# A planned order of work laid down with other lengths, and P V sets that may run in two halves

## The chip, the cores and the metric

The kernel runs on one core of a Trainium2 chip. The core has five engines with queues of their own: TensorE (PE in the profile, with PEld for its weight loads) for matmuls, ScalarE (ACT) for exponentials, VectorE (DVE) and GpSimd (POOL) for elementwise work, and SyncE (SP), which issues most DMAs. Matmuls write to PSUM, eight banks of 512 fp32 columns. The metric is the device time of one execution in microseconds. A difference of under about 0.2% can't be told from no change.

## The reference

Two attention blocks over the same input x (2048 tokens, 512 wide, 32 heads of 16) are mixed by a gate:

```python
x = A_x
g = _sigmoid((x * gate_w).sum(-1, keepdims=True))
# A: softmax attention
q, k, v = split((x @ A_wqkv))                       # 32 heads of 16
p = _softmax(einsum("bhqd,bhkd->bhqk", q, k) * 16 ** -0.5)
a = einsum("bhqk,bhkd->bhqd", p, v) @ A_wo
# B: linear attention
phi = lambda t: where(t > 0, t + 1, exp(t)) + 1e-6
num, den = phi(q) @ (phi(k)^T v), phi(q) . sum(phi(k))
b = (num / (den + 1e-6)) @ B_wo
return g * a + (1 - g) * b
```

Nearly all of the work is A's: 32 heads of 2048 x 2048 scores, each put through an exponential, and the product of the exponentials with V (called P V here).

## The kernel before, in words

**Units, groups and rounds.** The scores of a head are computed transposed: keys on the partitions, 512 queries along the columns. One unit is 128 keys by 512 queries of one head and fills one PSUM bank. A round is four heads by 512 queries, 64 units; there are 32 rounds, so 2048 units. Four 32-row strips of the array hold one head each, so one pass of PE (tiles `Qpad`, `KT`, line 685, where every matmul is issued) gives the scores of two to four units at once. ACT takes two banks at a time in one call (1024 columns, line 2063), and sometimes three (1536) or one (512). There are two slots of three banks each (`SLOTS`), used in turn: while ACT reads one, PE fills the other. The stretch of PE's work between two passes is called a gap here.

**Claims.** The third unit of a pass mostly isn't ACT's. It is claimed (`claim`): VectorE turns the scores into an integer whose bits are an approximate exponential (line 1565), and two more copies with an added step come from GpSimd (line 1609) or VectorE (line 1606). Three products with weighted V stand for the one exponential, so a claimed unit costs PE three products instead of one and ACT nothing. `MIN_LEFT`, `CLAIM_LOAD`, `RING_LOAD`, `STARVE` and `LATE` say when a claim may be made and when another step goes first.

**P V.** The products run in sets of four (`pv_cols`): four matmuls of 32 columns of weights, one for each head of the round, side by side in the array, 512 queries each, all into one accumulator bank. After the 64 units' worth of a round (`acc_n` reaches 64) the bank is copied out (`oraw`, line 1306), normalised, and another bank takes the next round. The last round runs in another form, full array and 52 columns, for a short end.

**Steps.** Everything else of PE (projections of Q, K and V, all of block B, the output products) is cut into steps and pieces that are put into gaps by `misc_step`, when their target group is due. Their results are evicted by VectorE, those with an exponential by ACT too (`epool`, line 970). The projection of Q, the normalisation, the transposes of B's output and the outputs issue DMAs on SP's queue.

**The order is written by a planner.** The program is straight-line code for each engine, in an order that the Python code plans as it records. It keeps a clock for each engine (`PE.t`, `AC.t`, `DV.t`, `PO.t`) from assumed lengths: `SET_T` of a set, `MM512` of a 512-wide matmul, `QK_T` of a pass, `SWITCH_T` where PE changes the way in which the array is divided, and so on. Nothing of these lengths is in the program: on the chip each engine runs its order as fast as its semaphores allow. A length that is off only puts work where it doesn't fit. After each pass the loop at lines 2092 to 2106 fills the gap:

```python
t_late = max(t_lim, AC.t - (QK_T + SWITCH_T + ROWS_SEEN + LAT + MARGIN))
...
room = min(MOST, int((t_late - PE.t - enter) / SET_T + ROOM))
if behind and room > 0 and pv_step(PE.t, most=room, least=3):
    continue
```

`t_late` is the latest time at which the next pass should come so that ACT doesn't run dry; `t_lim` is when its banks come free. `room` is the number of sets that fit, where a set may reach over the end by up to `ROOM` of its length. `least` is how many of the four columns of a set must be filled. `behind` is whether many exponentials wait for their product. Then steps have their turn, then sets again. If PE has nothing to do before `t_lim`, and too little was multiplied lately, `fill` puts in a matmul with zeros (`warm`), which keeps the clock of the array up.

Of the kernel before, what the change touches and what calls it, by code (L numbers as in the profile page):

```python
# [17 lines left out]
STATS = {}  # L18
# [167 lines left out]
LAT = 0.11  # L186
SET_T = 0.218
MM512 = 0.216
QK_T = 0.324
# [4 lines left out]
PV_MAC = 0.087  # L194
SWITCH_T = 0.095
SELF_T = 0.08
# [16 lines left out]
def bass_gated_mix__mha_block__linear_attn_block__prompt_kernel(  # L213
# [30 lines left out]
    PRE_GAP = 6  # L244
    OUT_GAP = 6

    with ExitStack() as es:
# [194 lines left out]
        ADD_W = 0.4  # L442
        YIELD = 1.2
        YIELD_SOON = 0.5
        POOL_TT = 1.3
# [892 lines left out]

        def pv_cols(now, r, force, want, most, least):

# [16 lines left out]
            sets = []  # L1357
            while len(sets) < most:
                s = [q[0] for q in by_j if q]
                full = sum(1 for j in range(4) if by_j[j] or left_j[j] == 0)  # L1360
                if not s or (full < least and not (force and any(e in first for e in s))):
                    break
                for q in by_j:
                    if q:
                        q.popleft()
                sets.append(s)
# [3 lines left out]
            t8 = rounds[r][0]  # L1370
            fns, rds = [], []
            for s in sets:
                STATS["sets"] = STATS.get("sets", 0) + 1
                STATS["in_sets"] = STATS.get("in_sets", 0) + len(s)
                for e in s:
# [10 lines left out]
                    for res in (e[3], vr):  # L1386
                        if res not in rds:
                            rds.append(res)
                    acc_n[0] += e[4]
                    done_j[(r, j)] = done_j.get((r, j), 0) + e[4]  # L1390
                    pv_pending.remove(e)
            pe_macro(fns, reads=rds, writes=[r_acc], dur=SET_T * len(sets), mac=0.2 * len(sets), mode="cols")
            fresh[0] = False
            if acc_n[0] == NU:
# [30 lines left out]

        def pv_step(now, force=False, want=None, most=3, least=4):

# [16 lines left out]
            if r < NR - 1 or part[0] == 0:  # L1444
                return pv_cols(now, r, force, want, most, least)
            if add_part(False):
                return True
            most = PV_UNITS * most
            sel = []
# [67 lines left out]

        MIN_LEFT = 14
        MIN_LEFT_LAST = 20
# [99 lines left out]
        GPR = 14.8  # L1619
        B0 = 0.4  # L1620
        B1 = 21
# [208 lines left out]
        FORCE_N = 1  # L1830
        MOST = 4
        OVER = 0.15
        FIRST_T = 0.43
        ROOM = 0.6
        CLAIM_LOAD = 3.2
        LATE_CLAIM = 4
        STARVE = 5
        MAC_LOW = 0.45
# [3 lines left out]
        END_FROM = 44  # L1842
        RING_LOAD = 4
        RING_LATE = 4
        BEHIND = 30
        LEND = 140
        RES_FROM = 60
        MARGIN = 0.19
        PV_LAG = 14
        LATE = 12  # L1850
        LAG_END = 12
# [128 lines left out]
        while True:  # L1980
# [112 lines left out]
            while PE.t < t_lim - 0.05:  # L2093
                pump(PE.t)
                behind = sum(1 for e in pv_pending if e[3] in r_PT) > (PV_LAG if act_round[0] < NR - 1 else LAG_END)
                enter = SWITCH_T if pe_mode[0] == "full" else 0.0
                room = min(MOST, int((t_late - PE.t - enter) / SET_T + ROOM))
                if behind and room > 0 and pv_step(PE.t, most=room, least=3):
                    continue
                if g > last_stage and misc_step(PE.t, t_late):  # L2100
                    continue
                if not behind and room > 0 and pv_step(PE.t, most=room):
                    continue
                if PE.t + FILL_T < t_lim and mac_until(max(t_lim, PE.t + FILL_AHEAD)) < (MAC_END if acc_n[0] >= END_FROM else MAC_LOW) and fill(PE.t):
                    continue
                PE.t += 0.05
# [248 lines left out]
```

## Time and profile before

| What | us |
|---|---|
| Time of the runs: median (lowest to highest) | 675.98 (675.3 to 675.98) |
| The profiled execution's own time | 675.2 |
| Its span, first to last instruction | 673.4 |
| ACT busy | 660.0 |
| PE busy | 655.0 |
| DVE busy | 576.0 |
| POOL busy | 550.8 |

The span is 1.8 us shorter than the execution's own time, which includes what lies around it. Busy time counts a moment once in which two calls of one engine overlap. So a busy engine may still be late: ACT's calls are longer in the records than the time from one to the next. For PE the ends of matmuls are modelled; starts are recorded. In the rows of groups and of the timeline, what stands in square brackets or behind the bar is the idle time just before, with what ended it.

### The profile page before, as it was taken

To read this page: it belongs to the slowest core of one execution; us is meant where nothing else is said; L and a number is where in the kernel's file an instruction comes from. 1 tells how busy PE (TensorE), PEld (TensorE's weight loads), DVE (VectorE), ACT (ScalarE), POOL (GpSimd) and SP (SyncE) were. 2 spreads that over 40 slices of the span, in tenths; PEclk is the share of its full clock that TensorE was granted. 3 is DMA by queue.
4 is the path that set the end of the run, shared out by engine and by line. 5 is a ranking of instruction groups with operands and counts; after the bars stand their busy time and mean duration, and the time that the engine had idled before them with its cause. 6 is when DMAs were issued, how large, how long until landed. Compare 5 with 4: busy or idle time off the path is not lost.

```text
span 673.4 us, 19207 instructions
## 1 busy us (share of the span) xinstructions
PE 655.0 (97%) x8078; PEld 200.1 (30%) x8080; DVE 576.0 (86%) x968; ACT 660.0 (98%) x715; POOL 550.8 (82%) x311
## 2 busy tenths in 40 slices
PE   8999999999999999999999999999999999999997
PEld 4322223333223232333222323323322222222223
DVE  4589889889887886888988998999889998989894
ACT  6999999999999999999999999999999999999995
POOL 5098889887889997788986999778788888898883
PEclk9999999999999999999999999999999999999999
DMA  9900101001010021101001010010211401010011
GB/s 221 252 3 12 24 2 31 6 11 27 1 35 2 18 50 35 32 2 29 7 10 35 10 41 11 16 29 13 46 26 24 52 25 42 10 44 24 20 41 44
DMA packets 44816, 22.96 MB, mean 34 GB/s; under 512 B 33976, under 2 KB 40568, under 8 KB 44728
## 3 DMA queue, kind: packets, MB, share of 16 engines
q1 hardware_dynamic: 42712, 20.12, 13.5%
q10 hardware_dynamic: 2016, 1.57, 0.9%
q8 instruction: 66, 1.08, 0.7%
q14 instruction: 22, 0.18, 0.1%
HBM read 8.00 MB, written 2.10 MB: 15 GB/s over the span
## 4 chain that ended last, share of the span: by engine, by line
ACT 95%; PE 4%; DMA 1%; DVE 1%; issue 0%; ACTq 0%
ACT PT L2063 92%; PE ps L685 3%; ACT epool L970 2%; DMA PT<-in_A_x_dram 1%; DVE DP L2165 0%; DVE xT L1909 0%; PE ps L692 0%; DVE KT L859 0%; DVE DP L2170 0%; DVE flag L2175 0%; ACT eg L954 0%; ACTq L2278 0%
## 5 line engine op out<-in xcount | busy, mean ns | idle before, releaser
L2063 ACT ACTIVATE PT<-ps 128x1024 bf16<-128x1024 f32 (+1 forms) x675 | 648.1, 1155 | 0.7 <-PE ps L685 0.5
L1609 POOL TENSOR_TENSOR DP<-DP,step 128x1024 int32<-128x1024 int32 x278 | 527.0, 1925 | 99.1 <-DVE DP L1565 27.6
L1565 DVE TENSOR_SCALAR DP<-ps 128x512 int16<-128x512 f32 x654 | 433.0, 685 | 69.1 <-PE ps L685 62.9
L685 PE MATMUL ps<-Qpad,KT 32*128 32x512 bf16 x2048 | 264.6, 384 | 10.0 <-ACT PT L2063 4.7
L685 PE MATMUL ps<-DP,Vaug 128*32 128x512 f16 x1949 | 206.8, 384 | 1.6 <-DVE oraw L1306 0.7
L685 PE MATMUL ps<-PT,Vaug 128*32 128x512 bf16 x1384 | 174.3, 384 | 0.6 <-DVE Vaug L914 0.5
L685 PEld LDWEIGHTS ps<-Qpad,KT 32*128 32x128 bf16 x2048 | 66.6, 91 | 269.9 <-ACT PT L2063 242.9
L685 PEld LDWEIGHTS ps<-DP,Vaug 128*32 128x32 bf16 x1949 | 49.7, 94 | 66.2 <-issue 41.1
L685 PEld LDWEIGHTS ps<-PT,Vaug 128*32 128x32 bf16 x1384 | 42.1, 95 | 46.7 <-issue 36.7
L685 PE MATMUL ps<-warm 128*32 128x512 bf16 (+1 forms) x272 | 46.7, 387 | 1.1 <-POOL step L735 1.1
L1606 DVE TENSOR_SCALAR DP<-DP 128x2048 int16<-128x2048 int16 (+1 forms) x50 | 33.4, 696 | 0.0
L685 PE MATMUL ps<-xT,wA 128*32 128x512 bf16 x432 | 32.6, 384 | 0.0
L1294 POOL TENSOR_TENSOR OT<-oraw,rbc 128x512 bf16<-128x512 f32 x12 | 15.6, 1302 | 11.3 <-DVE DP L1606 5.4
L970 ACT ACTIVATE epool<-ps 128x512 bf16<-128x512 f32 x32 | 23.4, 731 | 0.0
L1306 DVE COPY oraw<-ps 128x512 f32<-128x512 f32 x31 | 21.2, 682 | 0.7 <-PE ps L685 0.6
L685 PE MATMUL ps<-xT,wB 128*32 128x512 bf16 x256 | 19.7, 384 | 0.0
L685 PE MATMUL ps<-wB,xT 128*32 128x512 bf16 x256 | 19.3, 384 | 0.0
L685 PE MATMUL ps<-woA,OT 128*32 128x512 bf16 (+1 forms) x226 | 19.1, 384 | 0.0
L975 DVE SCALAR_TENSOR_TENSOR phi<-ps,epool 128x512 bf16<-128x512 f32 x24 | 16.3, 681 | 0.0
L685 PEld LDWEIGHTS ps<-warm 128*32 128x32 bf16 (+1 forms) x272 | 11.6, 98 | 13.8 <-issue 12.1
L859 DVE CAST KT<-ps 128x512 bf16<-128x512 f32 (+1 forms) x16 | 10.7, 667 | 5.2 <-PE ps L685 5.2
L685 PE MATMUL ps<-wA,xT 128*128 128x128 bf16 x192 | 14.9, 220 | 0.0
(106 smaller groups left out, 244.4 us busy)
## 6 DMA issues: line engine op xcount, KB each, us to landing
rbc<-oraw SPq DMA_DIRECT2D x16, 256.0 KB
OT<-in_A_x_dram SPq DMA_DIRECT2D x4, 512.0 KB, 7.1
Qpad<-Qs SPq DMA_DIRECT2D x124, 16.0 KB, 1.8
oraw<-oraw SPq DMA_DIRECT2D x60, 32.0 KB, 1.9
wA<-in_A_wqkv_dram SPq DMA_DIRECT2D x1, 1536.0 KB, 7.7
wB<-in_B_wqkv_dram SPq DMA_DIRECT2D x1, 1536.0 KB, 8.6
out_dram<-outt SPq DMA_DIRECT2D x12, 128.0 KB, 1.7
phi<-in_A_x_dram ACTq DMA_DIRECT2D x3, 256.0 KB, 6.1
```

What stands on the lines that cost most here:

```text
L685: return lambda: nc.tensor.matmul(o, lhsT=l, rhs=r, start=start, stop=stop, skip_group_check=sg)
L859: push(1, [(lambda: nc.vector.tensor_copy(KT[:, par, c0:c1], src), [r_bank[b]], [r_KT[par][t]], d_psum(n), None)])
L970: op(AC, lambda: nc.scalar.activation(epool[:, s, :], bank_ap(b), ACT.Exp), reads=[r_bank[b]], writes=[r_e[s]], dur=0.6, issue=0.48)
L975: (lambda: nc.vector.scalar_tensor_tensor(out=dst, in0=bank_ap(b), scalar=0.0, in1=epool[:, s, :], op0=ALU.max, op1=ALU.add), [r_bank[b], ...
L1294: push(1, [(lambda: (nc.gpsimd if on_pool else nc.vector).tensor_tensor(OT[:, t8, 512 * qc:512 * (qc + 1)], oraw[:, 0, :], rbc[:], ALU.mul ...
L1306: push(0, [(lambda: nc.vector.tensor_copy(oraw[:, half, :], acc), [r_acc], [r_oraw[half]], d_psum(512), evicted)])
L1565: push(0 if in_group else 1, [(lambda: nc.vector.tensor_scalar(DP[:, i, 512 * k:512 * (k + 1)].bitcast(I16), bank_ap(b), FRAC - Y_BIAS4, Y ...
L1606: ops = (lambda z=z, i2=i2, y=y, n=n: nc.vector.tensor_single_scalar(DP[:, i2, 0:n].bitcast(I16), y, STEPS[z], ALU.add), mine_, out_, d_sb ...
L1609: ops = (ops[0], mine_ + [r_step], out_, ops[3], None, POOL_ADD, lambda z=z, i2=i2, y=DP[:, i, 0:n].bitcast(I32), n=n: nc.gpsimd.tensor_te ...
L2063: op(AC, lambda p0=p0, b0=b0, n=n: nc.scalar.activation(PT[:, 512 * p0:512 * p0 + n], ps[:, 512 * b0:512 * b0 + n], ACT.Exp, scale=LN2 / F ...
```

## The change

The assumed lengths of a set, of a 512-wide matmul and of a switch are set to other values, and with them some twenty thresholds of the planner, so the whole order comes out anew. A set of P V may be run as two halves of 256 columns: where no whole set fits (`room` is 0) but 0.12 us less 40% do, `pv_cols` issues the first half and keeps the second in `split`, which runs when P V has its next turn. Only when the second half is issued are the products counted. The second call of `pv_step` in the loop no longer needs `behind` to be false, and takes sets with three filled columns where a whole set fits. `count` and `ended` hold what stood at the end of `pv_cols` before.

In numbers of the order that is laid down: 676 passes in place of 675, ACT calls of three, two and one banks 48, 628 and 0 in place of 45, 629 and 1, claims 648 in place of 654, P V sets 890 in place of 869, of which 103 run as halves, and filler groups 71 in place of 116.

```diff
--- before.py
+++ after.py
@@ -184,15 +184,15 @@
 
 
 LAT = 0.11
-SET_T = 0.218
-MM512 = 0.216
+SET_T = 0.223
+MM512 = 0.222
 QK_T = 0.324
 
 PVW = 26
 WIDE_MAC = 0.4
 PV_T = 0.1012
 PV_MAC = 0.087
-SWITCH_T = 0.095
+SWITCH_T = 0.104
 SELF_T = 0.08
 ROWS_SEEN = 0.0
 ACT_END = 0.25
@@ -242,7 +242,7 @@
     KV0, KV1 = 1.0, 1.2
     PRE_T = 5
     PRE_GAP = 6
-    OUT_GAP = 6
+    OUT_GAP = 4
 
     with ExitStack() as es:
         _cnt = [0]
@@ -440,8 +440,8 @@
         port_ev = [None]
         boost = [None]
         ADD_W = 0.4
-        YIELD = 1.2
-        YIELD_SOON = 0.5
+        YIELD = 1.8
+        YIELD_SOON = 0.3
         POOL_TT = 1.3
         POOL_V = 0.9
         POOL_ADD = 1.97
@@ -1336,7 +1336,19 @@
         done_j = {}
         PV_UNITS = 2
 
-        def pv_cols(now, r, force, want, most, least):
+        split = []
+        HALF_T = 0.12
+        ROOM_H = 0.4
+
+        def pv_cols(now, r, force, want, most, least, half=False):
+
+            if split:
+                s, fns, rds = split.pop()
+                pe_macro(fns, reads=rds, writes=[r_bank[acc_bank[0]]], dur=HALF_T, mac=0.1, mode="cols")
+                count(r, s)
+                return ended(r)
+            if half and most == 0 and len(started) < 4:
+                return False
 
             urgent = sum(1 for e in pv_pending if e[3] in r_PT) > PT_URGENT
             mine = [e for e in pv_pending if e[0] == r]
@@ -1355,7 +1367,7 @@
                 by_j[e[1] % 4].append(e)
             left_j = [16 - done_j.get((r, j), 0) - sum(e[4] for e in by_j[j]) for j in range(4)]
             sets = []
-            while len(sets) < most:
+            while len(sets) < max(most, half):
                 s = [q[0] for q in by_j if q]
                 full = sum(1 for j in range(4) if by_j[j] or left_j[j] == 0)
                 if not s or (full < least and not (force and any(e in first for e in s))):
@@ -1368,7 +1380,7 @@
                 return False
             acc, r_acc = acc_of(acc_bank[0]), r_bank[acc_bank[0]]
             t8 = rounds[r][0]
-            fns, rds = [], []
+            fns, rds, two = [], [], []
             for s in sets:
                 STATS["sets"] = STATS.get("sets", 0) + 1
                 STATS["in_sets"] = STATS.get("in_sets", 0) + len(s)
@@ -1386,10 +1398,27 @@
                     for res in (e[3], vr):
                         if res not in rds:
                             rds.append(res)
-                    acc_n[0] += e[4]
-                    done_j[(r, j)] = done_j.get((r, j), 0) + e[4]
-                    pv_pending.remove(e)
+                    if most == 0:
+                        two.append([f_mm(acc[32 * j:32 * j + 32, c:c + 256], w, p_ap[:, c:c + 256], start=False, stop=False, sg=True)
+                                    for c in (0, 256)])
+            if most == 0:
+                pe_macro([a for a, _ in two], reads=rds, writes=[r_acc], dur=HALF_T, mac=0.1, mode="cols")
+                split.append((sets[0], [b for _, b in two], rds))
+                STATS["halves"] = STATS.get("halves", 0) + 1
+                return True
             pe_macro(fns, reads=rds, writes=[r_acc], dur=SET_T * len(sets), mac=0.2 * len(sets), mode="cols")
+            for s in sets:
+                count(r, s)
+            return ended(r)
+
+        def count(r, s):
+            for e in s:
+                acc_n[0] += e[4]
+                done_j[(r, e[1] % 4)] = done_j.get((r, e[1] % 4), 0) + e[4]
+                pv_pending.remove(e)
+
+        def ended(r):
+            acc, r_acc = acc_of(acc_bank[0]), r_bank[acc_bank[0]]
             fresh[0] = False
             if acc_n[0] == NU:
                 assert r < NR - 1
@@ -1423,7 +1452,7 @@
                       for k in range(2) for qb in range(4)], reads=rd, writes=[r_bank[acc_bank[0]]], dur=0.5, mac=0.4)
             return True
 
-        def pv_step(now, force=False, want=None, most=3, least=4):
+        def pv_step(now, force=False, want=None, most=3, least=4, half=False):
 
             r = acc_round[0]
             if r >= NR:
@@ -1442,9 +1471,11 @@
             if fresh[0]:
                 started.clear()
             if r < NR - 1 or part[0] == 0:
-                return pv_cols(now, r, force, want, most, least)
+                return pv_cols(now, r, force, want, most, least, half)
             if add_part(False):
                 return True
+            if most == 0:
+                return False
             most = PV_UNITS * most
             sel = []
             if want is not None:
@@ -1515,7 +1546,7 @@
                 return None
             return r + 1
 
-        MIN_LEFT = 14
+        MIN_LEFT = 15
         MIN_LEFT_LAST = 20
 
         def can_claim(now, js):
@@ -1617,7 +1648,7 @@
 
         Q_OFF = -4
         GPR = 14.8
-        B0 = 0.4
+        B0 = 0.8
         B1 = 21
         chains = []
 
@@ -1828,26 +1859,26 @@
         HURRY = 40
         CLAIM_FREE = 1
         FORCE_N = 1
-        MOST = 4
+        MOST = 5
         OVER = 0.15
         FIRST_T = 0.43
-        ROOM = 0.6
-        CLAIM_LOAD = 3.2
+        ROOM = 0.4
+        CLAIM_LOAD = 3.5
         LATE_CLAIM = 4
-        STARVE = 5
+        STARVE = 6
         MAC_LOW = 0.45
         MAC_END = 0.45
         FILL_T = 0.2
         FILL_AHEAD = 0.9
         END_FROM = 44
-        RING_LOAD = 4
+        RING_LOAD = 3.8
         RING_LATE = 4
         BEHIND = 30
-        LEND = 140
-        RES_FROM = 60
-        MARGIN = 0.19
+        LEND = 100
+        RES_FROM = 59
+        MARGIN = 0.15
         PV_LAG = 14
-        LATE = 12
+        LATE = 8
         LAG_END = 12
         A_FIRST = 200
         LATE_END = 0
@@ -2095,11 +2126,15 @@
                 behind = sum(1 for e in pv_pending if e[3] in r_PT) > (PV_LAG if act_round[0] < NR - 1 else LAG_END)
                 enter = SWITCH_T if pe_mode[0] == "full" else 0.0
                 room = min(MOST, int((t_late - PE.t - enter) / SET_T + ROOM))
-                if behind and room > 0 and pv_step(PE.t, most=room, least=3):
+                half = room <= 0 and t_late - PE.t - enter > HALF_T * (1 - ROOM_H)
+                room = max(0, room)
+                if half and split and pv_step(PE.t, most=0, half=True):
+                    continue
+                if behind and (room > 0 or half) and pv_step(PE.t, most=room, least=3, half=half):
                     continue
                 if g > last_stage and misc_step(PE.t, t_late):
                     continue
-                if not behind and room > 0 and pv_step(PE.t, most=room):
+                if (room > 0 or half) and pv_step(PE.t, most=room, least=3 if room > 0 else 4, half=half):
                     continue
                 if PE.t + FILL_T < t_lim and mac_until(max(t_lim, PE.t + FILL_AHEAD)) < (MAC_END if acc_n[0] >= END_FROM else MAC_LOW) and fill(PE.t):
                     continue
```

## The prediction

> **What bounds the kernel now.** I read the page first, for the engines and the chain that ended last.
>
> ```profile
> PE 655.0 (97%) x8078; PEld 200.1 (30%) x8080; DVE 576.0 (86%) x968; ACT 660.0 (98%) x715; POOL 550.8 (82%) x311
> ...
> PEclk9999999999999999999999999999999999999999
> ...
> ACT PT L2063 92%; PE ps L685 3%; ACT epool L970 2%; DMA PT<-in_A_x_dram 1%; DVE DP L2165 0%; DVE xT L1909 0%; PE ps L692 0%; DVE KT L859 0%; DVE DP L2170 0%; DVE flag L2175 0%; ACT eg L954 0%; ACTq L2278 0%
> ```
>
> ACT's exponentials carry the chain, with TensorE (PE) as full beside them. The page seems to say that ACT never waits. That is an artefact: ACT's calls overlap in the records, so a late start leaves no idle time. The groups kept apart by shape and ACT's timeline, asked at single moments, show it.
>
> ```profile
> L2063 ACT ACTIVATE PT<-ps 128x1024 bf16<-128x1024 f32 x629 | 590.9, 1130 | 0.0
> L2063 ACT ACTIVATE PT<-ps 128x1536 bf16<-128x1536 f32 x45 | 65.1, 1517 | 0.6 <-PE ps L685 0.5
> L970 ACT ACTIVATE epool<-ps 128x512 bf16<-128x512 f32 x32 | 23.4, 731 | 0.0
> ```
>
> ```profile
> 9.18 1.45 ACT L2063 ACTIVATE PT<-ps 128x1536 bf16<-128x1536 f32 x1 [0.52 <-PE ps L685]
> ...
> 427.53 1.02 ACT L2063 ACTIVATE PT<-ps 128x1024 bf16<-128x1024 f32 x1
> ...
> 437.48 1.16 ACT L2063 ACTIVATE PT<-ps 128x1024 bf16<-128x1024 f32 x1
> ...
> 452.15 0.72 ACT L970 ACTIVATE epool<-ps 128x512 bf16<-128x512 f32 x1
> 452.62 1.16 ACT L2063 ACTIVATE PT<-ps 128x1024 bf16<-128x1024 f32 x1
> ...
> 639.63 25.38 ACT L2063 ACTIVATE PT<-ps 128x1024 bf16<-128x1024 f32 x25
> ...
> 657.66 5.52 ACT L2063 ACTIVATE PT<-ps 128x1536 bf16<-128x1536 f32 x4
> ```
>
> From 427.53 to 437.48 lie eleven two-bank calls without a stall: 9.95/11 = 0.904 us from start to start, while the mean record is 1.13 us. A three-bank call takes (5.52 - 1.53)/3 = 1.33 us (four in a row, the last one's own 1.53 off), an epool call 0.47 us. So ACT's work is 629 x 0.904 + 45 x 1.33 + 32 x 0.477, with 0.5 for one one-bank call: 644.3 us. The first call starts at 9.18 and the last ends at 639.63 + 25.38 = 665.01: 655.8 us. **ACT therefore stands still for 11.4 us that no idle column shows**, in small pieces. One place shows where they come from:
>
> ```profile
> 300.14 0.39 PE L685 MATMUL ps<-Qpad,KT 32*128 32x512 bf16 x3
> 300.47 0.61 PE L685 MATMUL ps<-OBT,OT 128*32 128x512 bf16 x8
> 301.01 0.39 PE L685 MATMUL ps<-Qpad,KT 32*128 32x512 bf16 x3
> 301.33 0.61 PE L685 MATMUL ps<-OBT,OT 128*32 128x512 bf16 x8
> 301.88 0.39 PE L685 MATMUL ps<-Qpad,KT 32*128 32x512 bf16 x3
> 302.20 0.83 PE L685 MATMUL ps<-PT,Vaug 128*32 128x512 bf16 x12
> 302.97 0.39 PE L685 MATMUL ps<-Qpad,KT 32*128 32x512 bf16 x3
> ```
>
> ```profile
> 301.50 1.02 ACT L2063 ACTIVATE PT<-ps 128x1024 bf16<-128x1024 f32 x1
> ...
> 302.41 1.03 ACT L2063 ACTIVATE PT<-ps 128x1024 bf16<-128x1024 f32 x1
> ...
> 303.41 1.02 ACT L2063 ACTIVATE PT<-ps 128x1024 bf16<-128x1024 f32 x1
> ```
>
> Between two passes of scores (Qpad,KT) lies a gap that PE fills with sets of four 32-wide matmuls. A gap of two sets takes 0.87 us from pass to pass (301.01 to 301.88), less than ACT's 0.904. A gap of three takes 1.09 (301.88 to 302.97), 0.18 more than ACT's. Behind the two-set gap ACT starts 0.53 after the pass (302.41), behind the three-set gap 0.44 (303.41), the shortest there is. So PE was 0.09 ahead, lost 0.18, and ACT's step became 1.00 instead of 0.904. Taking such differences for all 675 calls, 6.3 of the 11.4 us stand behind the 125 gaps of three sets (0.05 each), 2.6 behind the 340 gaps of two, and 2.5 behind the rest.
>
> **The change, part by part.** Counts of after are counts in its order of instructions.
>
> ACT's work: MIN_LEFT 14 to 15, CLAIM_LOAD, RING_LOAD and their like let VectorE claim 648 units instead of 654, so ACT does six more. Its calls become 628 + 48 + 0 in place of 629 + 45 + 1: -0.9 + 4.0 - 0.5 = **+2.6 us**, on the path.
>
> Halves: 103 sets run as two halves of 256 columns. Their price is read off the only 256-wide matmuls of before:
>
> ```profile
> L685 PE MATMUL ps<-xT,outt 128*32 128x512 bf16 x64 | 4.4, 381 | 0.6 <-DVE xT L1909 0.6
> ...
> L685 PE MATMUL ps<-xT,outt 128*32 128x256 bf16 x32 | 1.2, 274 | 0.0
> ```
>
> A 256-wide one is 0.107 shorter, half of the 0.215 by which the third set lengthened its gap. So two halves cost one set, and nothing is lost but the additional weight loads, which run beside the matmuls. The bounds are 0.107 and a full 0.215 for a half; I take 0.107, since this row is the same shape. The Trainium skill, "TensorE: Matmul & The Clock Gate", section "Wait — 56ns, not 53.3ns?", says that without hardware decode the sequencer spends about 62 ns on a matmul, which binds when the array's work is shorter. By it four matmuls of a half would take an estimated 0.25 us and a half would save nothing; the row above, 0.107 shorter for half the columns, speaks against it.
>
> Gaps: those of three sets fall from 125 to 41, those of two and a half rise from 6 to 95, those of two go from 340 to 350, and those with full-array work from 123 to 95. A gap of 2.5 sets takes 0.87 + 0.107 = 0.98: 0.07 longer than ACT's step, less than the 0.09 that PE is ahead. It stalls nothing by itself, and at most what three sets do, 0.05 on average. The 22 gaps of before that are 0.98 long, for other reasons, stall ACT by 0.016 each; I take that. By kind, after's stalls are 41 x 0.05 + 95 x 0.016 + 2.7 + 2.2 = 8.5 us.
>
> The plan's lengths: before planned a two-set gap at 0.324 + 2 x 0.218 + 0.095 = 0.855 where the rows have 0.87, so PE ran 0.015 later in each gap than the planner believed, until a wait brought them together. With 0.223 and 0.104 it plans 0.874. The latest planned pass hardly moves: MARGIN 0.19 to 0.15 allows 0.03 more (with SWITCH_T), ROOM 0.6 to 0.4 takes 0.04 away. So a three-set gap should stand more often where ACT can bear it. No row shows how often. The bounds are no credit (8.5) and only small pieces left, about 4; I take off half of the 3.6 us behind long gaps and 1.0 for the two-set gaps after them: **5.7 us of stalls, 5.7 fewer than now**.
>
> PE's sum: 45 fewer filler groups on `warm` save 9.7 us at 0.215; least=3 for sets while behind makes 890 sets of 869, 4.5 us more. PE gains 5 us, off the path but for what is priced as stalls. The new call of P V also runs while PE is behind on exponentials, so it may now wait for a product:
>
> ```profile
> PEld ps L685 <- POOL DP L1609: 10.2, 37, 0.5
> ```
>
> Behind such a wait the next pass is queued, and ACT behind that. The lower bound is none; the upper is another 10 us, if all of it fell before a pass that has no slack. I take zero, since it was there before within the 11.4, and GpSimd's additions fall from 278 to 265.
>
> VectorE gains eleven wide additions (0.7 each) and loses eight small operations: under 5 us more in 576 of 673, covered by its own idle time. The clock stays at full: fillers fall only where work takes their place. Starting times of B's steps (B0), output steps (OUT_GAP, 6 to 4) and lending (LEND) move their DMAs on SP's queue past the loads of Qpad; as many are issued as before, each planned ahead of its reader, so I cost them at zero, at most one wait of about 2 us.
>
> The end:
>
> ```profile
> 663.27 0.38 PE L685 MATMUL ps<-Qpad,KT 32*128 32x512 bf16 x1
> 663.76 0.96 PE L685 MATMUL ps<-Vaug,DP 128*128 128x52 bf16 x32
> ...
> 665.11 1.16 PE L685 MATMUL ps<-Vaug,PT 128*128 128x52 bf16 x40
> ...
> 667.50 0.40 PE L692 MATMUL ps<-identb,Osb 128*128 128x128 bf16 x4
> 667.73 1.72 PE L685 MATMUL ps<-woA,OT 128*128 128x512 bf16 x7
> ```
>
> After the last pass, the changed kernel has seven more 512-wide matmuls (0.22 each, of the seven in 1.72) and 20 fewer 52-wide ones (0.025): +1.0 before the transposes at 667.50. The last call is of two banks, 0.43 longer, which is in ACT's work already and covers part: **+0.6**, between 0 and 1.2.
>
> Sum: 2.6 - 5.7 + 0.6 = -2.5 on the profiled execution's 675.2, so 672.7. That execution stands 0.8 below the median of the runs, 675.98; I put the forecast at 673.4.
>
> **The rivals.**
>
> *The halves only shift the stalls* (no change). The kinds of gaps keep their prices and the plan's lengths bring nothing: stalls 8.5, so 2.6 - 2.9 + 0.6 = +0.3: 676.3. For it: PE is still 97% busy, so catching up takes long, 0.034 per two-set gap. Against it: the rows show that the old lengths were short in every gap.
>
> *The fuller gaps use up PE's lead* (slower). A gap of 2.5 sets loses 0.07, and it needs two gaps of two sets to win it back; in after's order 68 of them follow a two-set gap directly and few have three before. Where the lead is gone, each costs like three sets: 95 x 0.05 = 4.8 instead of 1.5, and the 41 gaps of three the full 0.095 of the place shown: 3.9 instead of 2.1. Stalls 8.5 + 3.3 + 1.8 = 13.6, so 2.6 + 2.2 + 0.6 = +5.4: 681.4. Milder, with stalls as now, +3.2: 679.2. It decides from stalls above 9.6 us. For it: ACT's 2.6 us are certain, the gain is not.
>
> *A half costs a set* (the change doesn't do what it says). Then 95 gaps are as long as those of three sets, and so are the 33 of one set and two halves: stalls 8.5 + 3.3 + 1.7 = 13.5, 681.3. The 256-wide row speaks against it.
>
> **How the numbers follow.** The forecast has 0.48, no shift 0.22, the lead used up 0.25, the half as a set 0.05. What a measurement can tell here is about 0.2%, 1.35 us. The first case is faster, the second is the same, the last two are slower. The range reaches from 670.3 (stalls of about 4 and an end without cost give 670.4 on the profiled scale, 671.2 on the median's, and a little under it for a lucky plan) to 679.6, which takes in the milder form of the slower rival; the first case alone spans 670.3 to 674.6.
>
> **What would show it.** Right: three-set gaps rare, passes 0.98 apart where a half lies between, ACT's first call to its last end about 653 us, fewer steps of 1.00. Wrong: an ACT interval over 656, PE's weight loads waiting longer for POOL or DVE, halves that last 0.2, or a clock below full in any slice.

## The result: no change that can be told, a little on the slow side

The changed kernel takes 676.91 us (median of 19 runs, 676.4 to 677.4), the kernel before 675.76 (19 runs, 674.99 to 676.36). The ratio is 1.0016, 95% interval 1.001 to 1.0023: 1.15 us (0.17%) slower. The interval leaves out 1, but a difference of under 0.2% counts as no change here. The forecast was 673.4 us and "faster"; the time lies inside the range of 670.3 to 679.6, but the sign is wrong.

The page of the changed kernel: busy times, the granted clock in 40 slices, and the chain that ended last by line.

```profile
PE 655.6 (97%) x8428; PEld 208.3 (31%) x8428; DVE 577.7 (86%) x971; ACT 660.8 (98%) x716; POOL 527.4 (78%) x298
...
PEclk9999999999999999999999999999999999999999
...
ACT PT L2094 74%; PE ps L685 21%; ACT epool L970 2%; DVE DP L1596 0%; POOL OT L1294 0%; PE ps L692 0%; DVE DP L2200 0%; DVE KT L859 0%; DVE oraw L1306 0%; DVE xT L1940 0%; DVE DP L1637 0%; DVE DP L2205 0%; DVE flag L2210 0%; POOL warm L733 0%; POOL dummy L702 0%
```

ACT is as busy as before, the clock is full, and PE now carries 21% of the chain instead of 3%. ACT's groups by shape and its timeline (start, length) at single moments:

```profile
L2094 ACT ACTIVATE PT<-ps 128x1024 bf16<-128x1024 f32 x628 | 593.9, 1241 | 0.0
L2094 ACT ACTIVATE PT<-ps 128x1536 bf16<-128x1536 f32 x48 | 71.9, 1612 | 0.7 <-PE ps L685 0.5
```

```profile
9.79 1.45 ACT L2094 ACTIVATE PT<-ps 128x1536 bf16<-128x1536 f32 x1 [0.53 <-PE ps L685]
...
121.54 1.31 ACT L2094 ACTIVATE PT<-ps 128x1024 bf16<-128x1024 f32 x1
...
122.51 1.26 ACT L2094 ACTIVATE PT<-ps 128x1024 bf16<-128x1024 f32 x1
...
123.43 1.26 ACT L2094 ACTIVATE PT<-ps 128x1024 bf16<-128x1024 f32 x1
...
665.02 1.33 ACT L2094 ACTIVATE PT<-ps 128x1024 bf16<-128x1024 f32 x1
```

The same calls are now 1.24 us long on average, 1.13 before. The length of a record is not ACT's work. That is the key to this case. The call at 122.51 starts 0.97 us after the one at 121.54, which by the prediction is 0.07 lost. But it ends at 123.77, and the one ahead of it at 122.85: 0.92 apart, like the next pair (124.69 - 123.77). Nothing was lost. **ACT's calls follow one another by their ends, 0.917 us apart for 1024 columns.** The starts can be closer, 0.904: in the records the next call begins before the one ahead has ended, and each record is some 0.0125 us longer than the last. A call that starts late merely gets a shorter record. Only when the record is down to 1.02 us, the length of a call with nothing ahead of it, does a later start move the end. All thirteen traces of this case bear this out: of their 8070 exponential calls of 1024 columns 193 end more than 0.93 us behind the call ahead, and the record of every one of these is 1.02 us long.

The two rows of before that gave the prediction its 0.904 say so as well: 427.53 + 1.02 = 428.55 and 437.48 + 1.16 = 438.64, eleven calls in 10.09 us, 0.917 each. I divided the distance of the starts and passed over the record's growth by 0.14.

Counted by ends (0.917 for two banks, 1.343 for three, 0.490 for one bank or an epool call):

| us | before | after |
|---|---|---|
| first exponential call ends | 10.63 | 11.24 |
| ACT's work behind it | 652.14 | 654.75 |
| real stalls (ends later than that work allows) | 2.24 | 0.36 |
| from ACT's last exponential end to the span's end | 8.44 | 8.96 |
| span | 673.4 | 675.3 |

For after: 628 x 0.917 + 47 x 1.343 + 32 x 0.490 and 0.08 for one small call (`eg`) are 654.75, and from 9.79 + 1.45 = 11.24 to 665.02 + 1.33 = 666.35 are 655.1. The first call's time differs by 0.6 between these two executions; over all profiled executions of this case that call begins anywhere from 9.2 to 10.0 with the same code ahead of it, so I don't count it. What is left is +2.61 - 1.88 + 0.52 = +1.25, beside the measured 1.15. The change did remove nearly all real stalls. There were only 2.2 us of them.

### The profile page after: what moved, and what is told of

Its sections match the earlier page's. It is cut to its first block, busy times and chain, and to the rows that moved or that the text cites. A ratio compares the mean times of both kernels' runs of the same rounds, so it can differ in the third digit from the quotient of the medians.

```text
span 675.3 us, 19878 instructions
## 1 busy us (share of the span) xinstructions
PE 655.6 (97%) x8428; PEld 208.3 (31%) x8428; DVE 577.7 (86%) x971; ACT 660.8 (98%) x716; POOL 527.4 (78%) x298
## 3 DMA queue, kind: packets, MB, share of 16 engines
q8 instruction: 69, 1.13, 0.7%
## 4 chain that ended last, share of the span: by engine, by line
ACT 77%; PE 21%; DVE 1%; POOL 0%; issue 0%; POOLq 0%; DVEq 0%; ACTq 0%
ACT PT L2094 74%; PE ps L685 21%; ACT epool L970 2%; DVE DP L1596 0%; POOL OT L1294 0%; PE ps L692 0%; DVE DP L2200 0%; DVE KT L859 0%; DVE oraw L1306 0%; DVE xT L1940 0%; DVE DP L1637 0%; DVE DP L2205 0%; DVE flag L2210 0%; POOL warm L733 0%; POOL dummy L702 0%
## 5 line engine op out<-in xcount | busy, mean ns | idle before, releaser
L1640 POOL TENSOR_TENSOR DP<-DP,step 128x1024 int32<-128x1024 int32 x265 | 503.8, 1930 | 124.2 <-DVE DP L1637 42.2
L1596 DVE TENSOR_SCALAR DP<-ps 128x512 int16<-128x512 f32 x648 | 428.3, 684 | 64.3 <-PE ps L685 60.4
L685 PE MATMUL ps<-DP,Vaug 128*32 128x512 f16 (+1 forms) x2263 | 216.4, 353 | 1.3 <-DVE oraw L1306 0.2
L685 PE MATMUL ps<-PT,Vaug 128*32 128x512 bf16 (+1 forms) x1464 | 171.6, 372 | 0.5 <-DVE Vaug L914 0.5
L685 PEld LDWEIGHTS ps<-DP,Vaug 128*32 128x32 bf16 x2263 | 58.5, 95 | 76.2 <-issue 49.6
L685 PEld LDWEIGHTS ps<-PT,Vaug 128*32 128x32 bf16 x1464 | 45.4, 95 | 40.2 <-issue 31.3
L1637 DVE TENSOR_SCALAR DP<-DP 128x2048 int16<-128x2048 int16 x59 | 39.5, 692 | 0.0
L685 PE MATMUL ps<-warm 128*32 128x512 bf16 (+2 forms) x214 | 36.8, 391 | 1.1 <-POOL step L735 1.1
L914 DVE CAST Vaug<-ps 128x512 bf16<-128x512 f32 x16 | 10.9, 683 | 2.9 <-PE ps L685 2.9
```

Of the source, the lines that this page charges most:

```text
L685: return lambda: nc.tensor.matmul(o, lhsT=l, rhs=r, start=start, stop=stop, skip_group_check=sg)
L914: ops = [(lambda: nc.vector.tensor_copy(v_group(NQC * par + v)[:, :, :, 0:16], src), [r_bank[b]], [r_V[par][v]], d_psum(512), lambda: v_do ...
L1596: push(0 if in_group else 1, [(lambda: nc.vector.tensor_scalar(DP[:, i, 512 * k:512 * (k + 1)].bitcast(I16), bank_ap(b), FRAC - Y_BIAS4, Y ...
L1637: ops = (lambda z=z, i2=i2, y=y, n=n: nc.vector.tensor_single_scalar(DP[:, i2, 0:n].bitcast(I16), y, STEPS[z], ALU.add), mine_, out_, d_sb ...
L1640: ops = (ops[0], mine_ + [r_step], out_, ops[3], None, POOL_ADD, lambda z=z, i2=i2, y=DP[:, i, 0:n].bitcast(I32), n=n: nc.gpsimd.tensor_te ...
```

## The experiments

The theory of ends says: the time is the sum of ACT's work counted by ends, of real stalls, and of what lies around; a late start costs nothing while the overlap lasts. Against it stand the prediction's own view (every start later than 0.904 is time lost) and its rivals (the fuller gaps use up PE's lead; a half costs a set). In the table that follows the experiments all kernels are counted in the same way. Real stalls are what is left over in that count, so its columns always add up; the tests are the kernels in which only PE or only ACT gets needless work. Nor does the count say how many real stalls a new order will have: in six of the eleven experiments the time came out above the range expected by the theory of ends, and each time with more real stalls than expected.

**PE made later by needless sets.** After every 16th (then every 8th) pass PE gets a set of four matmuls with zeros that the planner's clock doesn't count: 37 and 78 needless sets of 0.22 us. ACT's work is untouched.

```diff
+            if g > last_stage and g % SLIP == 0 and not fresh[0] and not r_bank[acc_bank[0]].pend and act_round[0] < NR - 1:
...
+                for j in range(4):
+                    ev = PE.add(f_mm(acc_of(acc_bank[0])[32 * j:32 * j + 32, :], warm[:, 0:32], warm4, start=False, stop=False, sg=True),
+                                _deps_for([r_warm], [r_bank[acc_bank[0]]]) if j == 0 else (), inc=(j == 3))
```

> The changed kernel with one needless set of four matmuls on zeros (0.22 us of PE) after every 16th pass of scores, 37 in all, put in after planning, so that nothing else in the order moves. Theory of starts (the prediction's: each late start of an ACT call is lost): PE leads by 0.02 to 0.09, so each costs ACT 0.13 to 0.20, about 5.5 us in all: 682.4. Theory of ends (ACT retires a two-bank call every 0.917 us whenever it was started within some 0.3 us; start to start may be 0.904 because calls overlap ever more in the records, and a late start only uses up that overlap): nothing to 1 us, 676.9 to 677.9, with the mean record of an ACT call shorter than now.

> As before, but after every 8th pass, some 75 sets, 16 us of PE in all. Theory of starts: 75 x 0.15 = 11 us, 688. Theory of ends: the overlap grows back by 0.0125 us a call, 0.1 in eight, and PE catches up 0.03 to 0.04 in each gap of two sets, so most is absorbed: 0 to 3 us, 677 to 680.

Groups by shape, first of the kernel with 37 sets, then of the one with 78:

```profile
L685 PE MATMUL ps<-warm 128*32 128x512 bf16 x316 | 34.8, 385 | 0.0
...
L2102 ACT ACTIVATE PT<-ps 128x1024 bf16<-128x1024 f32 x628 | 590.0, 1153 | 0.0
```

```profile
L685 PE MATMUL ps<-warm 128*32 128x512 bf16 x480 | 51.2, 386 | 0.0
...
L2102 ACT ACTIVATE PT<-ps 128x1024 bf16<-128x1024 f32 x628 | 590.8, 1098 | 0.3
```

Measured: 677.62 us (677.39 to 678.25), ratio 1.0031 [1.0021, 1.0042], and 680.93 (680.48 to 681.26), ratio 1.0073 [1.0057, 1.009]. The second is 0.9 above its expected range. The first 8.1 us of needless PE work cost 0.7 us, twice as much cost 4.0. The mean record of ACT falls from 1241 ns to 1153 and to 1098: lateness is taken out of the overlap first, and becomes time when the overlap is gone. Real stalls are 1.0 and 4.2, up 0.6 and 3.8 from the changed kernel's 0.4, which is nearly all of the added time.

**ACT made busier by needless calls.** Fifteen calls of 512 columns that nothing needs, spread over the kernel, likewise not counted by the planner.

```diff
+            if g > 60 and g % 40 == 0:
+                t_ac = AC.t
+                _emit(AC, lambda: nc.scalar.activation(extra[:], woA[:, 0, :], ACT.Exp), [r_woA], [r_extra], 0.6)
+                AC.t = t_ac
```

> The changed kernel with 15 needless ACT calls of 512 columns from SBUF, one after every 40th exponential call, put in after planning; PE's order is untouched. If ACT's retiring work is the bound (theory of ends), each lengthens the kernel by what it takes in ACT's row, 0.45 to 0.5 us: 15 x 0.48 = 7.2, 684.1. If PE, 97% busy, is the bound and ACT's overlap is slack, most of it is hidden: under 2 us, 678.9 at most.

```profile
L2096 ACT ACTIVATE PT<-ps 128x1024 bf16<-128x1024 f32 x628 | 598.2, 1253 | 0.0
...
L2102 ACT ACTIVATE extra<-woA 128x512 bf16<-128x512 bf16 x15 | 12.8, 852 | 0.0
```

Measured: 684.68 us (684.12 to 684.77), ratio 1.0129 [1.0115, 1.0144], 7.8 more than the changed kernel. By ends each extra call takes 0.507, 7.6 in all. ACT's work is on the path one to one, and PE's lateness is not while the overlap lasts. The groups' busy time tells the wrong thing here: it gives the fifteen calls 12.8 us.

**The change's parts alone.** First the changed kernel without halves; then the kernel before with only the three lengths of PE's work; then the kernel before with the halves, the looser second call of P V and all its old constants.

```diff
-                half = room <= 0 and t_late - PE.t - enter > HALF_T * (1 - ROOM_H)
+                half = False
```

> The changed kernel with halves never allowed, all else the same. The order comes out with 634 claims and ACT calls of two, three and one banks 612, 63 and 1. Theory of ends: ACT's work is 0.917 x (612-628) + 1.343 x (63-48) + 0.49 = +6.0 us against the changed kernel and its stalls stay under 1 us: 682.9, within 0.8. Theory of starts: work +6.0 too, stalls 7.5 by kinds of gaps (37 of three sets, 427 of two) in place of 9.3: 681.1. That the halves bring nothing: 676.9.

```diff
-SET_T = 0.218
-MM512 = 0.216
+SET_T = 0.223
+MM512 = 0.222
...
-SWITCH_T = 0.095
+SWITCH_T = 0.104
```

> The kernel before with nothing but the three lengths SET_T 0.223, MM512 0.222 and SWITCH_T 0.104. The order comes out with 637 claims, calls 611, 63, 0. Theory of ends: work +7.2 us against the kernel before, real stalls 2.2 down to about 0.4, end within 0.6: 681.1, within 1. Theory of starts: +7.2 and 3 fewer by kinds (58 gaps of three sets for 125), and with the credit the prediction gave for lengths that are right 3 more: 677 to 680.

```diff
-SET_T = 0.223
-MM512 = 0.222
+SET_T = 0.218
+MM512 = 0.216
...
-            ROOM = 0.4
-            CLAIM_LOAD = 3.5
+            ROOM = 0.6
+            CLAIM_LOAD = 3.2
...
```

> The code of the change with every constant set back to the kernel before: halves and the looser second call of P V are what is left of the change. The order comes out with 648 claims and ACT calls 616, 56, 0. Theory of ends: ACT's work +2.4 us against before; the old lengths leave its real stalls at some 2 us; the end has 3 more matmuls of 512 and 44 fewer of 52 columns, -0.4: 677.7, within 1. Theory of starts: work +2.4, stalls by kinds 10.5 for 11.4: 677.2. That halves by themselves take the stalls away: 675.5.

Measured: without halves 685.59 us (685.5 to 686.08), ratio 1.0144 [1.0127, 1.0161]; lengths alone 682.07 (681.2 to 682.25), 1.0089 [1.0072, 1.0105]; halves alone 679.26 (678.84 to 680.21), 1.0056 [1.0042, 1.0071]. Each of the three is slower than both whole kernels. The first and the last lie above what was expected by the theory of ends (682.9 and 677.7), as they have 2.9 and 4.4 us of stalls. Without halves 5.95 of the 8.7 us over the changed kernel are ACT's work: fewer units are claimed (634 instead of 648), and ACT does the rest. That the order claims less because PE falls behind in the planner's clock is argued, not shown. Of its stalls, 2.8 us lie in two places of one kind, each at the end of a round: 0.9 at 312.3 and 1.9 at 334.6. The second in PE's timeline, then in ACT's:

```profile
331.37 1.69 PE L685 MATMUL ps<-DP,Vaug 128*32 128x512 f16 x20
333.84 0.40 PE L685 MATMUL ps<-PT,Vaug 128*32 128x512 bf16 x4 [0.78 <-DVE oraw L1306]
```

```profile
334.61 1.02 ACT L2094 ACTIVATE PT<-ps 128x1024 bf16<-128x1024 f32 x1 [1.79 <-PE ps L685]
```

Twenty matmuls in a row without a pass, then a wait for the accumulator to be copied out; behind both stands the next pass. With halves alone ACT's work is 654.5, nearly as in the changed kernel, but stalls are 4.4: the new constants take away 4.0 of these and give back 1.4 behind ACT's last call (7.5 to 9.0). With the new constants the halves are worth some 6 us of ACT's work. With the old ones no gain shows: there the order with halves and the looser call gives ACT 2.4 us more than the kernel before does, and its stalls are 2.2 us more.

**ACT's own lengths put right.** The planner gave a call of n columns 0.055 + 0.000834 n us, which is close to the distance of starts (0.909 for 1024, where 0.904 was measured). Here it gets the distance of ends (0.917), with thresholds set anew, two orders that claim more:

```diff
-               dur=0.6, issue=0.48)
+               dur=0.6, issue=0.49)
...
-        MAC_LOW = 0.45
+        MAC_LOW = 0.423
...
-        MARGIN = 0.15
-        PV_LAG = 14
-        LATE = 8
+        MARGIN = 0.11
+        PV_LAG = 15
+        LATE = 10
...
-               dur=d_act(n), issue=0.055 + n * 8.34e-4)
+               dur=d_act(n), issue=0.0635 + n * 8.33e-4)
```

> The changed kernel with ACT's assumed lengths set to what it retires in (0.917, 1.343 and 0.49 us in place of 0.909, 1.336 and 0.48) and some fifteen thresholds chosen anew for that plan. The order: 650 claims, calls 615, 56, 0; 11 matmuls of 512 columns after the last pass, as in the kernel before, for 18. Theory of ends: work -1.2 us against the changed kernel, the end -0.5 to -1, real stalls 0.4 to 1: 675.0, 674.5 to 676.0, so within noise of the kernel before or a little faster. Theory of starts: work -1.1, stalls by kinds 7.9 for 9.3: 674.

The second differs from it in a few thresholds (MAC_LOW 0.42, B1 20.597, GPR 14.8, OUT_GAP 6, MARGIN 0.108).

> The same lengths, other thresholds: 653 claims, calls 619, 52, 1, so ACT's work is 2.4 us less than the changed kernel's and as large as that of the kernel before (+0.2). Theory of ends: 676.9 - 2.4 + 0.5 for PE's dearer gaps = 675.0, 674.3 to 676.2. If PE is the bound, more claims (three products for one) cost: over 677.

Measured: 677.85 us (677.57 to 679.87), ratio 1.0036 [1.0024, 1.0048], and 681.46 (679.72 to 683.58), 1.0082 [1.0066, 1.0098]. Both missed the 675.0. ACT's work did fall, by 1.2 and 2.4 us against the changed kernel, but in both profiled executions 3.0 us of stalls came up in one place. PE's timeline of the first and its windows of 1 us (window, its length, busy time of PE, PEld, DVE, ACT and POOL, granted clock, DMA share, GB/s):

```profile
184.26 0.40 PE L685 MATMUL ps<-xT,wA 128*32 128x512 bf16 x4 [1.62 <-DVE OBT L975]
```

```profile
182.00:183.00 1.00, 0.63 (x7) 0.11 (x6) 1.00 (x2) 1.00 (x2) 0.86 (x1) 1.00 0.00 0
183.00:184.00 1.00, 0.00 (x0) 0.00 (x0) 1.00 (x3) 0.69 (x1) 0.91 (x1) 1.00 0.05 16
184.00:185.00 1.00, 0.74 (x11) 0.22 (x11) 0.80 (x2) 0.00 (x0) 0.98 (x1) 1.00 0.00 0
...
187.00:188.00 1.00, 1.00 (x11) 0.21 (x9) 0.50 (x2) 0.55 (x2) 0.00 (x0) 0.50 0.06 16
```

PE stood still for 1.62 us, which cost ACT 1.7 us of stall; it was full again from 185, and then the granted clock went to half, from 186 to 189.4, which cost another 1.4. The clock did not fall in every execution: of the first kernel's six, four have a mean clock of 0.999 or 1.0 and take 677.57 to 677.86 us, and the two at 0.997 and 0.995 take 678.63 (the profiled one) and 679.87. Further stalls of 1.2 us near 337.5 in both and near 445 in the second stand behind pauses of PE of 1.29 and 1.50 us, in which it waited for VectorE's approximate exponentials (line 1596); the clock stayed full behind these.

In the second kernel 12.0 us lie behind ACT's last call instead of 9.0. The trace shows where: the last branch of PE's sequencer (line 2333), behind all of PE's work, takes 4.61 us, from 676.40 to 681.01, and 0.40 to 0.49 us in the other twelve traces. Every other engine is through with its own part by 678.2, so the branch makes that execution 3.0 us longer. What it waited for isn't shown.

**The same lengths with other thresholds.** MAC_LOW, MARGIN and the rest are the changed kernel's again; four others move. ACT's lengths are those of the last two kernels.

```diff
-               dur=0.6, issue=0.48)
+               dur=0.6, issue=0.49)
...
-    OUT_GAP = 4
+    OUT_GAP = 6
...
-        POOL_WAIT = 0.7
+        POOL_WAIT = 0.849
...
-        ROOM_H = 0.4
+        ROOM_H = 0.5
...
-        B0 = 0.8
+        B0 = 0.94
...
-               dur=d_act(n), issue=0.055 + n * 8.34e-4)
+               dur=d_act(n), issue=0.0635 + n * 8.33e-4)
```

> The changed kernel with ACT's assumed lengths set to the distances between ends (0.917 us for 1024 columns, 1.343 for 1536, 0.490 for 512) and five thresholds of the order set anew, so that ACT is given 625 calls of two banks, 47 of three and one of one bank, with 656 claims taken by DVE and GpSimd, against 628, 48 and 648 claims of the changed kernel. By the theory of ends ACT's work after its first call is 651.1 us (3.6 less than the changed kernel's 654.75 and 1.0 less than the 652.1 of before), real stalls 0.4 to 1.0, what lies behind ACT's last call 8.4: a median of 673.3 us, 672.5 to 674.5. Against it: if more claims tie up DVE or GpSimd so that PE runs dry once (as in the two kernels before it with new lengths), 3 to 5 us of stall come back in one place and the median is 676 to 679.

A second order, that one with LAG_END 11 in place of 12:

> As the kernel beside it, with a longer lead assumed for the last passes: 627 calls of two banks, 46 of three, 656 claims, and another order around the end. By the theory of ends ACT's work is 651.3 us, stalls 0.4 to 1.0, and the median 673.5 us, 672.5 to 674.8; with one place where PE runs dry, 676 to 679.

The page and the groups of the first, and its first and last call:

```profile
PE 653.1 (97%) x8472; PEld 209.9 (31%) x8472; DVE 582.9 (87%) x970; ACT 657.3 (98%) x713; POOL 550.6 (82%) x311
...
PEclk9999999999999999999999999999999999999999
...
ACT PT L2094 88%; PE ps L685 6%; ACT epool L970 2%; SPq L634 1%; DMA PT<-in_A_x_dram 1%; DMA rsum<-oraw 0%; DVE DP L2200 0%; DVE xT L1940 0%; DVE DP L1596 0%; PE ps L692 0%; DVE Qs L891 0%; DVE Vaug L914 0%; DVE KT L859 0%; DVE rraw L1279 0%; DVE DP L2205 0%
```

```profile
L2094 ACT ACTIVATE PT<-ps 128x1024 bf16<-128x1024 f32 x625 | 589.7, 1221 | 0.4 <-PE ps L685 0.4
L2094 ACT ACTIVATE PT<-ps 128x1536 bf16<-128x1536 f32 x47 | 70.4, 1611 | 0.7 <-PE ps L685 0.5
```

```profile
9.38 1.45 ACT L2094 ACTIVATE PT<-ps 128x1536 bf16<-128x1536 f32 x1 [0.53 <-PE ps L685]
...
662.04 0.87 ACT L2094 ACTIVATE PT<-ps 128x512 bf16<-128x512 f32 x1
```

Measured: 673.08 us (672.38 to 673.25), ratio 0.9958 [0.9945, 0.9972], and 673.12 (672.95 to 674.67), ratio 0.9967 [0.9955, 0.9979]; 673.3 and 673.5 were expected. **Both are faster than the kernel before and than the changed one.** From 10.83 to 662.91 are 652.1 us, of which 651.1 are work. How much of it is due to ACT's lengths and how much to the thresholds was not separated; that the same lengths with other thresholds took 677.85 and 681.46 us shows that the lengths alone don't do it.

**The new lengths and the halves with all old thresholds.**

```diff
-            MARGIN = 0.15
+            MARGIN = 0.19
...
-            LATE = 8
+            LATE = 12
...
```

> The changed kernel's lengths and halves with every threshold of the order as it was before: 604 calls of two banks, 66 of three, one of one bank, 641 claims. By the theory of ends ACT's work is 2.7 us more than the changed kernel's, 657.4, and with stalls of 0.4 to 1.5 the median is 679.6 us, 678.5 to 681. If the thresholds only shift stalls and the work given to ACT does not decide, it is within 1 us of the changed kernel, 676 to 678.

Measured: 682.89 us (682.04 to 684.01), ratio 1.0103 [1.0087, 1.0118], over the expected 678.5 to 681. ACT's work is 2.7 more than the changed kernel's, as expected; the stalls are 4.3 instead of the 0.4 to 1.5. In the profiled execution 1.9 us of them lie in one place, of the same kind as above. PE's timeline, its windows of 1 us, and ACT's timeline:

```profile
615.02 0.39 PE L685 MATMUL ps<-Qpad,KT 32*128 32x512 bf16 x3 [0.47 <-DVE DP L1596]
616.13 0.40 PE L685 MATMUL ps<-DP,Vaug 128*32 128x512 f16 x4 [0.71 <-DVE DP L1596]
```

```profile
614.00:615.00 1.00, 0.56 (x3) 0.10 (x2) 1.00 (x3) 1.00 (x2) 0.64 (x1) 1.00 0.00 0
615.00:616.00 1.00, 0.39 (x3) 0.12 (x3) 1.00 (x3) 0.99 (x2) 1.00 (x1) 1.00 0.00 0
616.00:617.00 1.00, 0.87 (x11) 0.32 (x15) 1.00 (x3) 0.58 (x2) 1.00 (x2) 0.95 0.00 0
617.00:618.00 1.00, 1.00 (x11) 0.10 (x3) 0.87 (x2) 0.92 (x1) 1.00 (x1) 0.50 0.02 3
...
620.00:621.00 1.00, 1.00 (x16) 0.22 (x11) 0.56 (x2) 0.89 (x2) 1.00 (x1) 0.84 0.00 0
```

```profile
616.90 1.02 ACT L2094 ACTIVATE PT<-ps 128x1024 bf16<-128x1024 f32 x1 [0.41 <-PE ps L685]
618.35 1.02 ACT L2094 ACTIVATE PT<-ps 128x1024 bf16<-128x1024 f32 x1 [0.42 <-PE ps L685]
619.87 4.41 ACT L2094 ACTIVATE PT<-ps 128x1024 bf16<-128x1024 f32 x4 [0.50 <-PE ps L685]
```

PE waits twice for VectorE's approximate exponentials. The waits use up ACT's overlap and cost 0.5 us, at the call of 616.90. At 616.90 the clock falls to half, until 620.32, and the next three calls end 1.3 us late in all. ACT's records are 1.02 long by then, and its idle column shows the stalls. The other 2.5 are in scattered places. Here too the clock differs between executions: the two with a mean clock of 0.997 take 683.39 and 684.01 us, the two with 0.999 and 1.0 take 682.04 and 682.38.

All kernels, counted by ends (us). All columns but the last are of the profiled execution; the last is the median of the runs. The profiled execution's own time is 1.8 us more than its span; where the clock fell in it (the first two rows of ACT's lengths, and old thresholds) it is 0.8 to 1.7 us above the median:

| | ACT's work | real stalls | behind ACT | span | median |
|---|---|---|---|---|---|
| before | 652.1 | 2.2 | 8.4 | 673.4 | 675.76 |
| after | 654.75 | 0.4 | 9.0 | 675.3 | 676.91 |
| 37 needless sets | 654.75 | 1.0 | 9.1 | 675.6 | 677.62 |
| 78 needless sets | 654.75 | 4.2 | 9.1 | 679.5 | 680.93 |
| 15 extra ACT calls | 654.75 | 8.0 (7.6 are the calls) | 9.0 | 683.0 | 684.68 |
| no halves | 660.7 | 2.9 | 9.4 | 684.3 | 685.59 |
| PE's lengths alone | 659.3 | 1.7 | 7.95 | 680.4 | 682.07 |
| halves alone | 654.5 | 4.4 | 7.5 | 677.2 | 679.26 |
| ACT's lengths, first | 653.6 | 4.8 | 7.7 | 676.8 | 677.85 |
| ACT's lengths, more claims | 652.4 | 6.2 | 12.0 (3.0 are the branch) | 681.4 | 681.46 |
| ACT's lengths, four thresholds | 651.1 | 0.9 | 8.4 | 671.3 | 673.08 |
| the same with LAG_END 11 | 651.15 | 0.3 | 9.0 | 671.1 | 673.12 |
| old thresholds | 657.4 | 4.3 | 9.15 | 682.2 | 682.89 |

## Why the prediction was wrong

- **The step that failed is "ACT therefore stands still for 11.4 us that no idle column shows".** ACT's work counted by ends is 653.5 us with its first call (1.45 + 652.1), by starts 644.3: these 9.2, some 0.013 a call, are overlap that grows and is used up, not time; real stalls were the other 2.2. So the credit of 5.7 us, the term that makes the forecast "faster", couldn't be had. The change took away 1.9, nearly all there was. In the prediction's own measure the changed kernel still "stands still" for 656.6 - 646.9 = 9.7 us, and loses only 0.4.
- ACT's work, +2.6: right (654.75 - 652.14 = 2.61), and on the path, as the extra calls show.
- The half at 0.107 and the gap of two and a half sets at 0.98: right. PE's timeline of the changed kernel, around the late start shown above:

```profile
121.10 0.39 PE L685 MATMUL ps<-Qpad,KT 32*128 32x512 bf16 x3
121.42 0.51 PE L685 MATMUL ps<-DP,Vaug 128*32 128x256 f16 x7
...
122.08 0.39 PE L685 MATMUL ps<-Qpad,KT 32*128 32x512 bf16 x2
```

  The passes are 0.98 apart; the median of the 92 such gaps that the trace shows whole is 0.979, that of the 33 of one set and two halves 0.877. The gap of two sets has 0.87, so the four matmuls of a half add some 0.107, or 0.027 each, and the rival of the half at a set's price falls. The rule of 62 ns per matmul without hardware decode ("TensorE: Matmul & The Clock Gate" of the Trainium skill, section "Wait — 56ns, not 53.3ns?") doesn't bind here.
- Its price of 0.016 per such gap and 0.05 per gap of three: wrong in kind. Where an overlap is left the price is zero. In the place that the prediction showed, the stall was real (ACT's records there are 1.02 and 1.03 long, the ends 303.44 and 304.43, 0.99 apart): I took the one place without overlap for all of them.
- The plan's lengths: the direction holds for the whole change. The changed kernel has next to no stalls, and its records are longer, so PE is further ahead. But PE's lengths alone take stalls only from 2.2 to 1.7 us and raise ACT's work by 7.2.
- PE's sum, POOL's and VectorE's waits, DMAs and clock at nothing: right for this order, as all of them together can be behind no more than the 0.4 us of stalls that are left in ACT's row. No slice shows a clock below full. The reason given for the 21 sets more isn't the code's: sets with three filled columns were allowed while behind in the loop before too; new is that the second call takes them as well.
- The end, +0.6: right (8.96 - 8.44 = 0.52). The transposes come at 669.37 where they were at 667.50, 3.02 behind ACT's last end instead of 2.49:

```profile
668.51 1.03 PE L685 MATMUL ps<-woB,OBT 128*128 128x512 bf16 x4
669.37 0.39 PE L692 MATMUL ps<-identb,Osb 128*128 128x128 bf16 x4
669.60 1.72 PE L685 MATMUL ps<-woA,OT 128*128 128x512 bf16 x7
```

- The rivals: "the halves only shift the stalls" came nearest in its time (676.3), and that is luck: it priced the stalls by starts, as the forecast did. Nothing was shifted; there was little to win. "The fuller gaps use up PE's lead" falls for this order. It has a true core, though: 78 needless sets do use up the lead, and from there on each costs.
- Of its signs, "an ACT interval over 656" was named for a wrong forecast, and it is 656.6. (A slip without weight: 672.7 and 0.8 make 673.5, where the forecast has 673.4.)

## What to carry to other kernels

Count the work of an engine whose records overlap from end to end, not from start to start and not by busy time; only where a record is down to its length without an overlap has a late start cost anything. Before crediting a change with removed stalls, work out how many real ones there are: here 2.2 us, and what counted beside them was the work that the order gives to ACT. The count tells what an order has cost, not what stalls the next order will have; in the places looked at above, those came mostly from PE waiting for VectorE. Of four orders planned with ACT's lengths counted by ends, two came out some 2.6 us faster than the kernel before and two 2.2 and 5.8 us slower; that such lengths make a better plan by themselves isn't shown.

## What the runs showed of the hardware

- ACT's calls from PSUM to SBUF end 0.917, 1.343 and 0.490 us apart for 1024, 1536 and 512 columns: 0.0635 us and 0.833 ns per column. The first call of a row is 1.02 us long at 1024 columns; with PE well ahead the records grow to 1.39 in the changed kernel. "ScalarE: Activation LUTs" of the Trainium skill, section "What ACT_TABLE_LOAD costs", gives the same 0.833 ns, but an overlap of about 93 ns between neighbours. Here the overlap is 0.10 at first and up to 0.47 (1.39 - 0.917).
- The granted clock fell to half for about 3.4 us after pauses of PE much shorter than that: 1.62 us in one kernel, 0.47 and 0.71 us close together in another, and only when PE had been at work again for 1.7 and 0.8 us. Behind single pauses of 1.50, 1.29 and 1.07 us in three other places it stayed full, and behind the pause of 1.62 us it seems to have fallen in two of six executions only, by their mean clock. So the length of a pause doesn't decide it by itself. "TensorE: Matmul & The Clock Gate" of the Trainium skill, section "What's actually happening", tells of a free-running window of 3.4 us over which activity is watched. The length of the slow stretch, 3.41 us in three traces, agrees with it. That section's table has the clock fall after an idle window; a wholly idle one was not needed here: in the 2 us from 614 to 616 PE was busy for 0.95.
